# A first retention sequence re-laid as token pairs: all its matmuls in 64x64 quadrants

## The chip, the core and the metric

The kernel runs on one core of one Trainium2 chip. Five engines take part, each with its own instruction stream that is worked off in order: PE (TensorE, the matrix engine; its weight loads are shown apart as PEld), DVE (VectorE), ACT (ScalarE), POOL (GpSimd) and SP (SyncE, which here only issues DMA transfers). The metric is the device time of one execution in microseconds (us); the time before is the median of three runs. A profiled execution is a further one, with its own time.

## The reference

There are three stages, and the output is the last one's. B=2 sequences, H=8 heads, S=768 tokens, D=64; the middle width is 512, the hidden width 2048.

```python
state = zeros(B, H, D, D)
for t in range(S):                                        # retention
    state = gamma[h] * state + k[:, :, t] (outer) v[:, :, t]
    y[:, :, t] = q[:, :, t] @ state / sqrt(D)
x = y.transpose(0, 2, 1, 3).reshape(1536, 512)
h = x @ moe_w_in;   x = where(h > 0, h, exp(min(h, 0)) - 1) @ moe_w_out
h = x @ moe2_w_in;  out = (max(h, 0) + log1p(exp(-abs(h)))) @ moe2_w_out
```

The weights come as 64-bit floats, and the kernel turns them into 32-bit ones with integer steps on ACT and DVE.

## The kernel before

**Stages.** Retention is done in chunks of 128 tokens: chunks 0 to 5 are the first sequence, 6 to 11 the second. The first layer works on three blocks of 512 tokens (four chunks each); a block has 16 units, each of 12 matmuls into a hidden tile (`H`, line 517) and 12 out of it (`R`, line 558). Before block 0 can start, chunks 0 to 3 must be through: this is the head, 0 to 27.3 us. Chunks 4 to 11 are spread between the units of block 0 and block 1, and the weights of layer one are loaded and converted while block 0 runs (27 to 105 us). The second layer follows (lines 696 and 751).

**One chunk j of the first sequence.** q and k, 128 tokens by 512, are transposed on PE against an identity (`Tq`, `Tk`, line 370, four matmuls each) and copied out of PSUM (`tq` on DVE, `tk` on ACT). The decay of q is multiplied in either ahead of the transpose (j = 0 and 1: `dq`, line 360, DVE) or as it is copied out (j = 2 to 5: line 391, DVE). `S` (line 437, eight matmuls, 64 rows by 128 columns of the array) makes the scores; `m` (line 447, DVE, two instructions) masks them; `O` (lines 474 and 480) adds what the carried state gives to what the masked scores give; `ST` (line 417) makes the chunk's share of the state and `st` (lines 426 to 429, DVE) the next state, which `sp` (line 402, POOL) spreads over a zeroed tile `wide` so that line 474 can use the whole array. `dv` (POOL, line 363) decays v. `xh` (ACT) and `xl` (DVE) split the result in two for the first layer. Every fp32 matmul of the program is two instructions on PE: the trace says x16 where the program has eight.

**Order and queues.** The order on all engines is one written list of steps, `TABLE`; `ct`, `cl`, `cj`, `cs` in it convert one weight tile, `ih`, `il`, `oh`, `ol` split one, `ar` to `gl` are the activation of a unit, `kc` issues filler matmuls on PE (line 240). All loads are issued by SP in the list's order. In the head the steps take PSUM banks in turn from a ring of seven (`banks`), afterwards from two.

Of the kernel before, what the change touches and what calls it, by code (L numbers as in the profile page):

```python
# [20 lines left out]
DVE_TILES = 8  # L21
TABLE = """
ST.5 ST.11 sp.7 st.5 sp.6 sp.8 Tq.8 Tk.8 sp.9 Tq.9 Tk.9 sp.10 Tq.10 Tk.10 sp.11 Tq.11 Tk.11 st.11 Lq.0 Lk.0 Lk.1 Lq.1 Lv.0
Lv.1 Lk.2 Lq.3 dq.0 Lq.2 Tq.0 kc.3 Lg.0 tq.0 Tk.0 Lv.2 Tk.1 tk.0 tk.1 S.0 Lk.3 dq.1 Lv.3 Tq.1 dv.0 m.0 kc.2 ST.0 Lw.0 dv.1
tq.1 O.0 st.0 Lk.4 sp.1 S.1 xh.0 Lq.4 xl.0 Tk.2 Lw.1 m.1 ST.1 tk.2 Tq.3 Lw.2 Tq.2 st.1 O.1 tq.2 sp.2 Lv.4 tq.3 S.2 Lq.5 dv.2
xh.1 xl.1 Lw.3 dv.3 ST.2 m.2 Tk.3 tk.3 st.2 O.2 Lw.4 sp.3 ct.0 Lk.5 cl.0 S.3 xh.2 cj.0 Lv.5 xl.2 Tk.4 tk.4 m.3 Lg.1 cs.0 O.3
ct.1 ih.0 Lw.5 cl.1 il.0 few xh.3 ST.3 cj.1 dv.4 ct.2 xl.3 Tq.4 cl.2 cs.1 Lq.6 H.0 st.3 ih.1 tq.4 sp.4 Lw.6 il.1 cj.2 S.4
ct.3 cs.2 ar.0 Lw.7 ih.2 H.1 m.4 ae.0 cl.3 il.2 ct.4 dv.5 cl.4 ab.0 cj.3 Tq.5 gh.0 O.4 Lq.7 cj.4 ar.1 cs.3 ae.1 gl.0 Lw.8
oh.0 H.2 cs.4 xh.4 ol.0 ct.5 ab.1 ih.3 cl.5 tq.5 gh.1 il.3 R.0 Lb.64 ar.2 cj.5 ae.2 xl.4 ct.6 cs.5 cl.6 Lw.9 gl.1 oh.1 H.3
cj.6 ct.7 ol.1 cl.7 cs.6 ab.2 ih.4 cj.7 Tk.5 Lb.65 gh.2 ST.4 il.4 tk.5 R.1 ct.8 cs.7 cl.8 st.4 Lk.6 oh.2 gl.2 sp.5 ar.3 ol.2  # L30
ct.9 cj.8 cl.9 S.5 Lw.11 ae.3 Lw.10 cs.8 Lw.14 cj.9 H.4 ih.5 Lw.12 ab.3 cs.9 gh.3 Lv.6 m.5 oh.3 R.2 ol.3 ar.4 gl.3 Lw.13
ae.4 il.5 ct.11 ab.4 cl.11 R.3 gh.4 cj.11 gl.4 ct.10 cl.10 cs.11 Lk.7 cj.10 oh.4 Tk.6 cs.10 H.5 tk.6 ol.4 Lw.16 ih.6 il.6
Lw.15 dv.6 O.5 ar.5 ae.5 ab.5 H.6 ct.13 Lb.66 cl.13 ct.12 cj.13 cl.12 cs.13 Lv.7 xh.5 cj.12 gh.5 R.4 oh.5 xl.5 ct.14 cs.12
cl.14 Lb.67 ol.5 ih.7 gl.5 ar.6 Tq.6 il.7 ct.15 tq.6 Lw.17 ae.6 H.7 cj.14 cl.15 dv.7 ab.6 ct.16 cs.14 gh.6 Lb.68 cj.15 ih.8
S.6 gl.6 cl.16 il.8 ar.7 R.5 Lw.18 cs.15 ae.7 Lw.19 m.6 oh.6 Lw.20 ct.17 ab.7 cl.17 Lb.69 ol.6 gh.7 H.8 cj.16 cj.17 cs.16
cs.17 ih.9 O.6 gl.7 ct.18 il.9 oh.7 cl.18 ol.7 ST.6 ar.8 cj.18 Lb.70 xh.6 R.6 st.6 ae.8 cs.18 ct.19 xl.6 ih.10 ab.8 Lw.22
# [15 lines left out]
R.21 ae.23 il.25 ct.35 m.10 ab.23 H.24 gh.23 oh.23 gl.23 ol.23 O.10 ar.24 ih.26 ae.24 il.26 ab.24 ST.10 xh.10 gh.24 R.22
xl.10 st.10 gl.24 H.25 oh.24 ol.24 R.23 ar.25 ih.27 ae.25 il.27 ab.25 H.26 gh.25 oh.25 gl.25 ol.25 R.24 ar.26 ih.28 ae.26
il.28 ab.26 H.27 gh.26 oh.26 gl.26 ol.26 S.11 ar.27 ih.29 R.25 ae.27 il.29 m.11 ab.27 H.28 gh.27 oh.27 gl.27 ol.27 O.11 end
yh.0.0 ar.28 yl.0.0 ih.30 ae.28 il.30 yh.0.1 ab.28 R.26 xh.11 yl.0.1 gh.28 xl.11 gl.28 H.29 oh.28 ol.28 R.27 ar.29 ih.31
ae.29 il.31 ab.29 H.30 gh.29 oh.29 gl.29 ol.29 R.28 ar.30 ih.32 ae.30 il.32 ab.30 cs.32 H.31 gh.30 oh.30 Lw.36 gl.30 cl.34
# [65 lines left out]
def tile_retention_elu_softplus(  # L122
# [708 lines left out]
```

## Time and profile before

| | us |
|---|---|
| median of three runs (lowest, highest) | 576.35 (576.28, 576.6) |
| the profiled execution | 576.78 |
| its span, first to last instruction | 575.1 |
| PE busy in it | 568.2 |
| DVE, ACT, POOL busy in it | 451.9, 371.7, 27.9 |

A busy share is a mean over the whole span; what a stage is bound by is read from the stage. Matmuls overlap in the engine, so the length of one is no measure of its cost: the cost of a group is the distance from its start to the start of the next. In the chain of waits that distance stands as the length of a piece.

### The profile page before, as it was taken

Reading aid. Unit: us, or ns where it says so; the run is one execution under the profiler, and the core shown is the slowest. Engines: PE = TensorE matmul, PEld = TensorE weight load, DVE = VectorE, ACT = ScalarE, POOL = GpSimd, SP = SyncE. Lnnn points to the kernel's source line nnn. Section 1 sums busy time; section 2 is a strip of 40 time slices with the busy share of each in tenths; the row PEclk is TensorE's granted clock in tenths of the full one; section 3 lists DMA queues with packets and bytes.
Section 4 is the critical chain, followed back from the end, with each engine's and each line's share of the span. In section 5 each row is a group of like instructions: output and inputs, shape, how many; then the busy total and the mean of one; then the engine's idle time right before and its main releaser. Section 6 shows DMA issues by size and latency. Waiting matters only on the chain.

```text
span 575.1 us, 8682 instructions
## 1 busy us (share of the span) xinstructions
PE 568.2 (99%) x3236; PEld 484.8 (84%) x3236; DVE 451.9 (79%) x785; ACT 371.7 (65%) x678; POOL 27.9 (5%) x37
## 2 busy tenths in 40 slices
PE   8999999999999999999999999999999999999997
PEld 5888888788888888888888998998998988998995
DVE  3899899996566466999999999877789876666653
ACT  2588888865565455888999875545566655554442
POOL 3221202020010000000000000000000000000000
PEclk9999999999999999999999999999999999999999
DMA  9997676732270001406776000000000200000002
GB/s 199 270 293 218 179 217 169 207 60 53 40 191 2 0 1 55 129 0 190 217 219 216 2 1 0 1 0 2 0 1 0 111 2 0 1 1 1 0 1 109
DMA packets 75834, 48.29 MB, mean 84 GB/s; under 512 B 53520, under 2 KB 69904, under 8 KB 75792
## 3 DMA queue, kind: packets, MB, share of 16 engines
q1 hardware_dynamic: 75504, 47.46, 30.4%
q8 instruction: 25, 0.41, 0.3%
q10 hardware_dynamic: 288, 0.28, 0.1%
q14 instruction: 17, 0.14, 0.1%
HBM read 44.58 MB, written 3.15 MB: 83 GB/s over the span
## 4 chain that ended last, share of the span: by engine, by line
PE 89%; DVE 5%; ACT 2%; DMA 2%; issue 1%; DVEq 0%; ACTq 0%
PE psb L751 23%; PE psb L696 21%; PE psb L558 20%; PE psb L517 20%; PE psb L437 2%; PE psb L370 1%; DVE cl L284 1%; DVE wl L306 1%; DMA raw<-moe_w_out 1%; PE psb L417 1%; DVE wi L293 1%; ACT wh L300 1%; DMA early<-q 1%; DVE wo L293 1%; DVE A L447 1%
## 5 line engine op out<-in xcount | busy, mean ns | idle before, releaser
L751 PE MATMUL psb<-wo,g 128*128 128x512 f32 x576 | 142.1, 392 | 0.0
L751 PEld LDWEIGHTS psb<-wo,g 128*128 128x128 f32 x576 | 107.5, 188 | 19.4
L517 PE MATMUL psb<-x,wh 128*128 128x512 f32 x384 | 96.0, 392 | 0.8 <-DVE st L428 0.6
L517 PEld LDWEIGHTS psb<-x,wh 128*128 128x128 f32 x384 | 71.5, 188 | 16.5 <-ACT cl L279 1.0
L696 PE MATMUL psb<-op,wx 128*128 128x384 f32 x336 | 67.0, 339 | 0.0
L696 PEld LDWEIGHTS psb<-op,wx 128*128 128x128 f32 x336 | 60.2, 188 | 2.5
L306 DVE TENSOR_TENSOR wl<-wi,wh 128x512 fp32r<-128x512 f32 x48 | 32.9, 685 | 32.9 <-ACT wh L300 32.8
L721 ACT ACTIVATE hx<-hx 128x384 f32<-128x384 f32 x64 | 33.2, 520 | 37.5 <-DVE hx L717 37.4
L558 PE MATMUL psb<-gh,wh 128*128 128x512 f32 x192 | 56.0, 398 | 0.0
L558 PE MATMUL psb<-gh,wl 128*128 128x512 f32 x192 | 54.4, 390 | 0.0
L558 PE MATMUL psb<-gl,wh 128*128 128x512 f32 x192 | 54.3, 389 | 0.0
L517 PE MATMUL psb<-x,wl 128*128 128x512 f32 x192 | 51.3, 389 | 0.0
L525 ACT ACTIVATE e<-psb 128x512 f32<-128x512 f32 x48 | 28.3, 589 | 30.2 <-PE psb L517 30.1
L274 ACT ACTIVATE cm<-raw 128x512 f32<-128x512 f32 x64 | 42.6, 665 | 5.1 <-DVE wi L293 2.9
L731 ACT ACTIVATE g<-hx 128x384 fp32r<-128x384 f32 x64 | 33.2, 520 | 19.0 <-DVE hx L725 18.9
L284 DVE SCALAR_TENSOR_TENSOR cl<-cm,cl 128x512 int32<-128x512 int32 x64 | 43.8, 693 | 2.0 <-ACT cl L279 1.9
L669 DVE TENSOR_TENSOR wo<-wo,wo 128x512 fp32r<-128x512 f32 x32 | 22.0, 687 | 29.6 <-ACT wo L665 29.6
L536 ACT ACTIVATE gh<-e 128x512 fp32r<-128x512 f32 x48 | 30.1, 628 | 21.4 <-DVE e L532 21.2
L279 ACT ACTIVATE cl<-raw 128x512 int32<-128x512 uint32 x64 | 42.5, 664 | 1.6 <-DVE wi L293 1.1
L558 PEld LDWEIGHTS psb<-gh,wl 128*128 128x128 f32 x192 | 36.1, 188 | 7.6
L558 PEld LDWEIGHTS psb<-gl,wh 128*128 128x128 f32 x192 | 36.0, 188 | 7.5
L517 PEld LDWEIGHTS psb<-x,wl 128*128 128x128 f32 x192 | 36.1, 188 | 7.5
(102 smaller groups left out, 894.0 us busy)
## 6 DMA issues: line engine op xcount, KB each, us to landing
raw<-moe_w_in SPq DMA_DIRECT2D x32, 512.0 KB, 4.7
raw<-moe_w_out SPq DMA_DIRECT2D x32, 512.0 KB, 4.4
out_dram<-o SPq DMA_DIRECT2D x11, 256.0 KB, 2.1
early<-q SPq DMA_DIRECT2D x4, 256.0 KB, 4.9
early<-k SPq DMA_DIRECT2D x4, 256.0 KB, 5.0
early_v<-v SPq DMA_DIRECT2D x4, 256.0 KB, 5.1
qb<-q SPq DMA_DIRECT2D x64, 16.0 KB, 2.0
qb<-k SPq DMA_DIRECT2D x64, 16.0 KB, 1.9
```

What stands on the lines that cost most here:

```text
L274: nc.scalar.activation(out=m, in_=raws[i][:, :, :, 1].bitcast(F32), func=AF.Copy, scale=2.0 ** -112)
L279: nc.scalar.activation(out=l, in_=raws[i][:, :, :, 0].bitcast(U32), func=AF.Copy, scale=2.0 ** -29 * (1 - 2.0 ** -12), bias=-0.499)
L284: nc.vector.scalar_tensor_tensor(out=l, in0=m.bitcast(I32), scalar=3, in1=l, op0=ALU.logical_shift_left, op1=ALU.bitwise_or)
L306: nc.vector.tensor_tensor(out=l, in0=wf[f][o], in1=ws[u, o][0].bitcast(F32), op=ALU.subtract)
L517: nc.tensor.matmul(b, w[:, kk, :], x[:, kk, :], start=(n == 0), stop=(n == len(seq) - 1))
L525: nc.scalar.activation(out=e, in_=hb[u], func=AF.Relu, scale=-1.0)
L536: nc.scalar.activation(out=gh, in_=acts[u], func=AF.Copy)
L558: nc.tensor.matmul(acc[i], st[:, i * P:(i + 1) * P], mv, start=(fresh and p == 0), stop=(f == NF - 1 and p == 2))
L696: nc.tensor.matmul(bank_p[b], w[:, h, k], x[l][:, k], start=(start and i == 0), stop=(i == len(seq) - 1), skip_group_check=True)
L721: nc.scalar.activation(out=e, in_=e, func=AF.Softplus)
L731: nc.scalar.activation(out=t[:, 0], in_=hid[Q, c][1], func=AF.Copy)
L751: nc.tensor.matmul(sums2[s], t[:, x, i * P:(i + 1) * P], o[:, w], start=(left[s] == 0 and p == 0), stop=(left[s] == 2 * NQ - 1 and p == 2) ...
```

## The change

It touches chunks 0 to 5 alone, and the order of everything.

- **Layout.** q, k and v of the first sequence are loaded so that one partition holds two neighbouring tokens of four heads (partitions 0 to 63 heads 0 to 3, the others heads 4 to 7). The pieces in memory are 512 bytes, before 256; each tile is two DMAs instead of one.
- **Quadrants.** `Tq`, `Tk`, `S`, `O` and `ST` are matmuls of 64 rows by 64 columns of the array, written so that four neighbours in the order fall on its four quarters. `Tq` and `Tk` are now plain matmuls, 16 for each tile, k against a folded identity `fold`, q against `scale_q`, the same with q's decay in it, made once (`dq`, DVE). `dq` of chunks 0 and 1 and the multiplication of line 391 are gone for the first sequence; `tq` of chunks 1 to 5 is two plain copies of half the size on ACT.
- **State.** The state needs no `wide`: `sp` is gone, and the state's part of `O` is two groups of four matmuls, one ahead of time (`X`) and one in `O`. `ST` writes into the same two banks as `O`. A tiny DVE copy `y` (128x4, `seen`) stands between `X` and `O`.
- **Halves.** `m` and `O` are split in halves, so that the first half of `O` can follow the first half of `m`.
- **Banks.** In the head the steps take pairs of banks by the list `PAIRS`. The pair (h0, h1) is among them; H.0 and H.1 write there.
- **Fillers.** The five later filler matmuls are gone, the first seven remain. `TABLE` is new throughout.

```diff
-            nc.sync.dma_start(out=t, in_=src)
+            src = heads.rearrange("(g h) (p e) d -> g p h (e d)", g=2, e=2)
+            for g in range(2):
+                nc.sync.dma_start(out=t[g * D:(g + 1) * D].rearrange("p (h e) d -> p h (e d)", e=2), in_=src[g])
...
+PAIRS = (0, 2, 4, 6, 0, 2, 4, 6, 0, 2, 6, 4, 0, 2, 4, 6)
...
-    def decay_query(j):
-        nc.vector.tensor_tensor(out=qkv[0, j], in0=qkv[0, j], in1=gt, op=ALU.mult)
+    def decay_diagonals():
+        nc.vector.tensor_tensor(out=scale_q, in0=fold.unsqueeze(1).to_broadcast([P, H, D]), in1=rates(H + HP, H), op=ALU.mult)
...
+        if j < CPB:
+            key = ("t", j, n if j == 0 else 0)
+            first = key not in bank
+            b = bank[key] if not first else pair(key)
+            for c in range(HP):
+                for g in range(2):
+                    for a in range(2):
+                        r, o, h = slice(g * D, (g + 1) * D), a * D, HP * a + c
+                        nc.tensor.matmul(b[o:o + D, g, (n * HP + c) * D:(n * HP + c + 1) * D], qkv[n, j][r, h, :],
+                                         fold[r] if n else scale_q[r, h, :], start=(first and c == 0), stop=(c == HP - 1), skip_group_check=True)
...
+                if j:
+                    for g in range(2):
+                        nc.scalar.activation(out=x[:, g], in_=y[:, g], func=AF.Copy)
+                else:
+                    nc.vector.tensor_copy(x, y)
...
-    def spread_state(j):
-        if j % CPB and j < CPB:
-            for i in range(2):
-                r = slice(i * D, (i + 1) * D)
-                nc.gpsimd.tensor_copy(wide[j % 2][r, :, r], states[j][r])
...
+    def carry(j, x):
+        b, qT = bank["o", j], qkT[0, j]
+        for a in range(2):
+            for c in range(2):
+                r, i = slice(a * D, (a + 1) * D), a ^ x
+                nc.tensor.matmul(b[c * D:(c + 1) * D, i, a * P:(a + 1) * P], states[j][r, 2 * i + c, :], qT[r, 2 * i + c, :],
+                                 start=(x == 1), stop=False, skip_group_check=True)
...
+    def settle(j):
+        x = seen[j] = rp.tile([P, 2, 2], F32, tag="seen", name="seen")
+        nc.vector.tensor_copy(x, bank["o", j][:, :, 0:2 * P:P])
```

What the new list makes of the order is seen at three places. The first is PE's stream around chunk 2's output in the head. `early` and `early_v` are the tiles that hold the loaded q, k, v and the transposed q and k of chunks 2 and 3, `wide` and `st` the state, `A` the masked scores, `psb` PSUM; the counts are those of the program. Before:

```order
L370 MATMUL psb<-ident,early 128x128 x8
L474 MATMUL psb<-qT,wide 128x128 x4
L480 MATMUL psb<-A,early_v 64x128 x8
L437 MATMUL psb<-early_v 128x128 x8
L417 MATMUL psb<-early_v,early 64x64 x8
L370 MATMUL psb<-ident,early 128x128 x4
L474 MATMUL psb<-early_v,wide 128x128 x4
```

And now:

```order
L488 MATMUL psb<-qT,st 64x128 x4
L555 MATMUL psb<-A,early_v 64x128 x16
L448 MATMUL psb<-early_v,early 64x64 x16
L507 MATMUL psb<-early_v 64x128 x16
L488 MATMUL psb<-early_v,st 64x128 x4
L390 MATMUL psb<-fold,early 64x64 x16
L390 MATMUL psb<-scale_q,early 64x64 x16
```

Where the state's matmuls stood together ahead of the scores' (line 474, 480), the state's are now four ahead of the next chunk's transposes and four behind them, and the next chunk's scores (line 507) follow the state's share at once.

The second place is PE's stream where the first layer begins (line 517 before, 592 now; `x_234` and `x_350` are block 0's tokens, `wh` and `wl` the two parts of a weight tile). Before:

```order
L474 MATMUL psb<-early_v,wide 128x128 x4
L480 MATMUL psb<-A,early_v 64x128 x8
L417 MATMUL psb<-early_v,early 64x64 x8
L370 MATMUL psb<-ident,q 128x128 x4
L517 MATMUL psb<-x_234,wh 128x512 x4
L517 MATMUL psb<-x_234,wl 128x512 x4
L517 MATMUL psb<-x_234,wh 128x512 x4
L437 MATMUL psb<-qT,kT 128x128 x8
```

And now:

```order
L390 MATMUL psb<-scale_q,q 64x64 x16
L488 MATMUL psb<-early_v,st 64x128 x4
L555 MATMUL psb<-A,early_v 64x128 x16
L448 MATMUL psb<-early_v,early 64x64 x16
L507 MATMUL psb<-qT,kT 64x128 x16
L488 MATMUL psb<-qT,st 64x128 x4
L592 MATMUL psb<-x_350,wh 128x512 x4
L592 MATMUL psb<-x_350,wl 128x512 x4
```

The scores of chunk 4 (line 437, now 507) and the first half of its carried part stood behind H.0 and now stand ahead of it.

The third place is DVE's stream in the head from chunk 2 on (`cl` and `cm` belong to the conversion of a weight tile, `wi` is its result). Before, from `tq` of chunks 2 and 3 on:

```order
L391 TENSOR_TENSOR early_v<-psb,gq_94 128x512 x2
L499 TENSOR_TENSOR x_234<-psb,x_234 128x4x128
L447 TENSOR_TENSOR A<-psb,mask 128x512 x2
L428 TENSOR_TENSOR st<-psb,st 128x256
L429 TENSOR_TENSOR st<-st,dec 128x256
L284 SCALAR_TENSOR_TENSOR cl<-cm,cl 128x512
```

And now, from the mask of chunk 3 on:

```order
L523 TENSOR_TENSOR A<-psb,mask_e 128x512
L572 TENSOR_TENSOR x_350<-psb,x_350 128x4x128
L497 COPY seen<-psb 128x4
L298 SCALAR_TENSOR_TENSOR cl<-cm,cl 128x512
L523 TENSOR_TENSOR A<-psb,mask_e 128x512
L307 SCALAR_TENSOR_TENSOR wi_122<-raw,cl 128x512
```

The multiplication of q is gone from it, the halves of the mask stand apart, and two steps of the weights' conversion stand between and behind them.

## Rows read from the trace of the kernel before

**Rows 1.** The page, part 1: busy time, share of the span and instructions by engine
```profile
PE 568.2 (99%) x3236; PEld 484.8 (84%) x3236; DVE 451.9 (79%) x785; ACT 371.7 (65%) x678; POOL 27.9 (5%) x37
```

**Rows 2.** Busy times by stage, its length first, cut where the text cuts
```profile
core 0: us, PE busy (x) PEld busy (x) DVE busy (x) ACT busy (x) POOL busy (x), PEclk, DMA share, GB/s
0.00:9.25 9.25, 7.25 (x24) 3.86 (x24) 2.35 (x4) 1.88 (x2) 2.46 (x11) 1.00 0.96 176
9.25:27.30 18.05, 17.86 (x247) 15.46 (x247) 13.16 (x23) 7.68 (x14) 6.54 (x10) 1.00 1.18 254
27.30:105.30 78.00, 77.19 (x529) 62.63 (x529) 75.36 (x121) 65.29 (x117) 11.33 (x10) 1.00 0.78 216
105.30:209.00 103.70, 103.70 (x703) 84.74 (x704) 70.08 (x113) 60.18 (x110) 7.59 (x6) 1.00 0.30 69
```

**Rows 3.** Who PE waited for, whole run, microseconds, times, longest
```profile
PE psb L370 <- DVE early L360: 0.7, 1, 0.7
PE psb L517 <- DVE st L428: 0.6, 1, 0.6
PE psb L437 <- DVE qT L391: 0.2, 1, 0.2
```

**Rows 4.** The chain that ended last, first 110 us: start, length, what
```profile
0.81 3.51 DMA early<-q
...
7.54 1.71 PE psb L370 x8
9.25 1.09 PE psb L437 x16
...
14.55 0.62 PE psb L417 x16
...
16.19 0.89 PE psb L474 x8
17.08 1.02 PE psb L480 x16
...
34.61 0.44 PE psb L370 x4
```

**Rows 5.** PE in order of time at 100 us: start, length, work
```profile
99.77 0.67 PE L459 MATMUL psb<-qT,st 64*64 64x128 f32 x16
100.26 0.41 PE L463 MATMUL psb<-A,v 64*64 64x64 f32 x16
100.60 0.69 PE L466 MATMUL psb<-A,v 128*64 128x64 f32 x16
```

**Rows 6.** PE in order of time at the head
```profile
1.26 3.17 PE L240 MATMUL psb<-warm 128*128 128x512 bf16 x7 [1.26 <-DVE warm L234]
...
9.18 1.16 PE L437 MATMUL psb<-qT,kT 64*128 64x128 f32 x16
...
27.26 1.20 PE L517 MATMUL psb<-x,wh 128*128 128x512 f32 x4 [0.18 <-ACT x L495]
```

**Rows 7.** VectorE in order of time at the head
```profile
10.44 1.29 DVE L447 TENSOR_TENSOR A<-psb,mask 128x512 f32<-128x512 f32 x2 [1.80 <-PE psb L437]
...
15.79 0.42 DVE L429 TENSOR_TENSOR st<-st,dec 128x256 f32<-128x256 f32 x1
16.22 1.29 DVE L391 TENSOR_TENSOR early_v<-psb,gq 128x512 f32<-128x512 f32 x2
```

**Rows 8.** Groups by line to 105 us, VectorE first, then ScalarE
```profile
L360 DVE TENSOR_TENSOR early<-early,dec 128x512 f32<-128x512 f32 x2 | 1.4, 692 | 4.1 <-DMA early<-q 4.1
L389 DVE COPY qT<-psb 128x512 f32<-128x512 f32 x2 | 1.4, 685 | 1.3 <-PE psb L370 1.3
...
L387 ACT ACTIVATE kT<-psb 128x512 f32<-128x512 f32 x6 | 3.6, 592 | 7.9 <-PE psb L370 7.9
```

**Rows 9.** Two stretches of the head, the DMA rate last
```profile
5.00:12.00 7.00, 6.83 (x57) 5.16 (x59) 2.97 (x6) 1.19 (x2) 2.08 (x2) 1.00 1.32 219
27.00:32.00 5.00, 4.58 (x31) 3.51 (x31) 4.93 (x9) 3.13 (x6) 2.54 (x3) 1.00 1.15 297
```

More of the change, by code (lines that the diff above doesn't have):

```diff
@@ L27 @@
[L27 to L36, printed above, removed]
@@ L52 @@
[L52 to L56, printed above, removed]
@@ L210, in tile_retention_elu_softplus @@
     dec = const.tile([P, 3 * H + 2 * HP], F32, name="dec")
-    gq = [const.tile([P, HP * P], F32, name=f"gq{n}") for n in range(2)]
+    gq = const.tile([P, HP * P], F32, name="gq")
+    scale_q = const.tile([P, H, D], F32, name="scale_q")
     nc.scalar.dma_start(out=dec, in_=decay)
@@ L318, in psum @@
     def psum(tag):
-        assert tag not in live
+        assert tag not in live, (tag, live)
         return psb[:, names.index(tag)]
-    banks = ["h0", "h1", "a0", "a1", "a2", "r0", "r1"]
+    banks = []
+    pairs = list(PAIRS)
     turn = [0]
@@ L349, in release @@
         return bank.pop(key)
-    wide = [rp.tile([P, HP, P], F32, tag="qb", name="wide") for i in range(2)]
-    for w in wide:
-        nc.gpsimd.memset(w, 0.0)
     qkT = {}
@@ L423, in next_state @@
         s = rp.tile([P, HP, D], F32, tag="st", name="st")
-        bb = release(("s", j))[:, 0:HP * D].rearrange("p (h d) -> p h d", h=HP)
+        if j < CPB:
+            bb = bank.pop(("s", j)).rearrange("p i (c d) -> p i c d", c=2)
+            out, old, rate = (None if x is None else x.rearrange("p (i c) d -> p i c d", i=2)
+                              for x in (s, states.get(j), dec[:, H:H + HP].unsqueeze(2).to_broadcast([P, HP, D])))
+            users[j] -= 1
+            if not users[j]:
+                release(("o", j))
+        else:
+            bb = release(("s", j))[:, 0:HP * D].rearrange("p (h d) -> p h d", h=HP)
+            out, old, rate = s, states.get(j), gs[1]
@@ L442, in causal @@
         if j < TPB:
-            a = [gp.tile([P, HP, P], F32, tag=t, name="A") for t in ("gh", "gl")]
+            a = gp.tile([P, HP, P], F32, tag=("gh", "gl")[i], name="A")
         else:
-            a = [ap.tile([P, HP, P], F32, tag=t, name="A") for t in ("A0", "A1")]
-        for i in range(2):
-            nc.vector.tensor_tensor(out=a[i], in0=bs[i].rearrange("p (h t) -> p h t", h=HP),
-                                    in1=(mask_t if i and j >= CPB else mask).unsqueeze(1).to_broadcast([P, HP, P]), op=ALU.mult)
@@ L449, in causal @@
-        scores[j] = a
-    def attend(j):
+            a = ap.tile([P, HP, P], F32, tag=("A0", "A1")[i], name="A")
+        m = mask_e.rearrange("p k t -> p (k t)") if j < CPB else mask_t if i else mask
+        n = 2 if j < CPB else HP
+        nc.vector.tensor_tensor(out=a.rearrange("p (c k) t -> p c (k t)", c=n), in0=bs[:, i].rearrange("p (c t) -> p c t", c=n),
+                                in1=m.unsqueeze(1).to_broadcast([P, n, HP // n * P]), op=ALU.mult)
+        scores.setdefault(j, []).append(a)
@@ L452, in attend @@
+    def attend(j, half=0):
         vt, qT = qkv[2, j], qkT[0, j]
-        a = scores.pop(j)
+        a = scores[j]
+        b = bank.get(("o", j)) if j in seen or half else pair(("o", j))
+        users[j] = 1
         if j >= CPB:
-            b = pair(("o", j))
             quads = [(i, pr, pr % 2 * D, pr // 2 * P) for n in range(0, HP, 2) for i in range(2) for pr in (n, n + 1)]
```

324 lines of the change are left out of this document (189 added, 135 removed).

## The prediction

> **What bounds the kernel now.** The views were read in this order. The page's busy times first: PE is busy 568.2 us of a span of 575.1 [rows 1], so the time is PE's work plus some 7 us. The table by stage next: between 27.3 and 105.3 us PE is busy 77.2 of 78.0, but DVE also 75.4 and ACT 65.3; from 105.3 to 209 us PE is alone, DVE has 70 of 104 [rows 2]. Then PE's waits: apart from the start there are three, 0.7 us before the first transpose, 0.6 us for a state of the second sequence (this one is at 105 us), 0.2 us for a transposed q behind H.0 [rows 3]. So the kernel ends when PE's work ends, DVE is close behind PE until 105 us, and a microsecond less of PE work counts fully only where DVE and ACT can follow. The profiled execution took 576.78 us, 1.68 more than its span; the median of the runs is 576.35. I sum against 576.78 and take the difference off 576.35.
>
> **Prices of the quadrant matmuls.** The second sequence already has them: 16 instructions of 64x64 with 128 columns take 0.49 us from their start to the next group's (99.77 to 100.26), 16 with 64 columns 0.34 (100.26 to 100.60) [rows 5]. Behind the second the shape of the array changes, behind the first it doesn't. I take 0.44 for the first, a little under the row since the 0.49 has a shape change at its own start. For the second the bounds are 0.22 (half, by columns) and 0.34 (the row); I take 0.235, near the lower one, since at the end of the 0.34 PE goes over to another shape, and inside the head this no longer happens: all groups are 64x64.
> Per chunk, in calls of two instructions each:
> - transposes of q and k: before 2 x 0.44 where nothing else is paid (34.61), more at most places [rows 4]; now 32 calls, 64 instructions with 64 columns, 4 x 0.235 = 0.94. Nothing gained, perhaps 0.1 lost.
> - scores: before 1.09 [rows 4]; now 16 calls with 128 columns, 0.87. Gain 0.2.
> - output: before 0.89 + 1.02 [rows 4]; now 8 calls for the state (0.44) and 16 for the scores (0.87). Gain 0.6.
> - state: before 0.62 [rows 4]; now 16 calls with 64 columns, 0.47. Gain 0.15.
> So 4.5 us a chunk become 3.6. It is the joined shapes and the half-empty `wide` that pay, not the transposes.
>
> **The head, followed as a chain.** With less PE work the head is no longer filled by PE; I follow the waits by hand. From PE's last score matmul to the mask DVE needs 0.1 us behind the row's end (9.18 + 1.16 to 10.44), that is 0.3 us after PE could go on; two masks take 1.29, `st` with both its steps 0.9 (to 16.22), a plain ACT copy 0.6 [rows 6, 7, 8]. Before, S.0 starts at 9.18 and H.0 at 27.26 [rows 6].
> Now: the fillers end at 4.2 [rows 6], k's first tile is there by then (the first q, 256 KB, landed at 4.3 when it was first in the queue [rows 4]; now a tile is two halves and k is ahead). Two transposes at the slow pace, 0.94 each, end at 6.2; `scale_q` is made meanwhile and hides behind Tk.0. tq.0 on DVE 6.55 to 7.25, S.0 at 7.3. From there each chunk needs 3.6 us of PE plus what it waits: X.j waits for `st` of the chunk before, which ends 1.2 us after ST while S.j covers 0.87 of it, so 0.3 to 0.4 us are lost a chunk. That puts S.1 at 11.1, S.2 at 14.8, S.3 at 18.8 (allowing 0.3 for a slow S.0). In the fourth round two things are added. Tk.4 takes the pair of banks that xl.2 still reads, and on DVE xl.2 stands behind st.2 and the first mask of chunk 3: PE waits until 21.3. And m.3.1, st.3 and xl.3 stand behind conversion steps of the first weights on DVE: O.3 ends at 23.4, ST.3 at 23.8, S.4 at 24.7, X.4 waits for st.3 until 25.1, and H.0, which writes the bank that o.3 lies in, waits for xl.3, until 26.3. Against 27.26 that is 0.95 us earlier, with more done: S.4 and half of chunk 4's carry already lie behind it.
>
> **Behind H.0.** Before, PE still has of the first sequence S.4 1.09, O.4 1.91, ST.4 0.62, the transposes of chunk 5 0.9, S.5 1.09, O.5 1.91: 7.5 us. Now: the rest of O.4 1.09, ST.4 0.47, transposes 0.94, S.5 0.87, X.5 and O.5 1.3: 4.7. Gain 2.8. The shape changes towards the first layer's matmuls are about as many as before (S.4, O.4, ST.4, S.5, O.5 against X.4, O.4 with ST.4, transposes, S.5, O.5), so they count zero. The two waits behind H.0, 0.2 and 0.6, fall away if DVE keeps up: gain 0.8.
>
> **Can DVE and ACT follow?** DVE loses two `dq` of 0.69, one of two copies of line 389, and four multiplications of line 391 (0.65 each from the pair), and gains `scale_q` and five tiny copies, which I bound by zero and 0.4 each and take at 0.15 [rows 7, 8]: about 3 us less. ACT gains five `tq`, between 0.6 and 0.8 each: 3.5 us. DVE had 2.6 us of slack in the 78 us to 105.3 [rows 2]; PE will need some 74.4 us for the same stretch, DVE about 74.4 of work. That is tight, but DVE starts it with work already done: in the head it was idle 11.7 of 27.3 us [rows 2], and the weights come earlier, since the loads of 256-byte pieces ran at 219 GB/s with the DMA engines full, and the mixed stretch later at 297 [rows 9]; for pieces of 512 bytes I take between the two. Following R.0 to H.5 by hand I find PE not waiting. I allow 0.4 us (bounds 0 and 3).
>
> **POOL and SP.** `sp` and `wide` go from POOL, two masks come; all hidden, v's decay now has POOL to itself. SP issues 18 DMAs more; the first ones took 0.43 us each to issue, and 36 halves at that price are as fast as the data, so zero, with 1 us as the worst.
>
> **Sum.** 0.95 + 2.8 + 0.8 - 0.4 = 4.2 us. 576.78 - 4.2 = 572.6 for the profiled execution, 576.35 - 4.2 = 572.2 us for the median.
>
> **Rivals.**
> 1. The head overlaps better than my chain (waits of 0.3 vanish, Tk.4 and H.0 aren't held by xl.2 and xl.3). Then PE's work alone counts: 15 us from S.0 at 7.3, H.0 at 22.3 to 23.5. Gain up to 3 us more: 569. For it: DVE and ACT have room in the head; against: the two bank waits are in the program.
> 2. The gain turns into waits on DVE and ACT before 105 us. For it: DVE is 97% busy there and ACT gets more [rows 2]; against: the idle head. Price: PE gains no more than DVE sheds, 2 to 3 us less a late conversion: 574.5.
> 3. Small quadrants are bound by issue and weight loads, not by columns: 0.34 for 16 everywhere [rows 5]. Twelve transposes and five states at 0.2 us more each are 3.5 us on PE, about 2.5 of them on the path: 574.5. A sentence from the Trainium skill, "TensorE: Matmul & The Clock Gate" (Wait — 56ns, not 53.3ns?), says that start-to-start never drops below about 25 ns however few the columns; an estimate from it is 0.8 us for each 32 instructions, which would take the whole gain. Here 16 starts take 0.34, 21 ns each with the shape change in it, so the trace doesn't bear it out.
> 4. Slower: the clock. The granted-clock column reads 1.00 throughout [rows 2], yet eight transposes took 1.71 us at 7.54, 0.21 each, and four took 0.44 later, 0.11 each [rows 4]: until about 9.2 us PE ran at the pace of the 1.2 GHz level, then at that of 2.4. Before it rose PE had been busy without a gap since 5.2, with three fillers in it. Now it has gaps of 0.3 to 1.1 us from 6.2 on and no fillers. If the pace stays low, each chunk has 2.7 us more on the chain; after a chunk and a half (at about S.2) the gain is gone, and through the whole head it costs 8 to 12 us: 580. Against it: the fillers now run straight into the transposes, 1.3 to 6.2 without a gap.
>
> **How the numbers follow.** Forecast (570.5 to 573.8) 0.48; rival 1 0.17; rival 2 0.17; rival 3 0.07; rival 4 0.11. A measurement tells about 0.2%, 1.15 us, from no change. Faster by more, under 575.2: the forecast, rival 1, most of 2, half of 3, 0.81. Within: the ends of 2 and 3 and a short rival 4, 0.10. Slower: the rest of rival 4, 0.09. The range leaves out rival 4 and the ends of 1 and 2: 568.5 to 575.8.
>
> **What would show it.** Right: S.0 near 7.3, S.1 to S.3 at steps of 3.7 to 4.0, H.0 at 26 to 27 with a wait for xl.3 before it, groups of 0.87 for the scores, transposes of 0.47, and no PE wait over 0.5 us between 27 and 100. Wrong: transposes of 0.65, scores that still take 1.7 us beyond 10 us, PE waiting for DVE lines 298 to 320 between 40 and 70 us, or H.0 at 23.

## The result: slower, and where the time went

The changed kernel takes 584.72 us (median of 4 runs, 584.07 to 586.3) against 576.48 of the kernel before on the same chip, a ratio of 1.0146 (95% interval 1.0122 to 1.017). The forecast was 572.2, with a range of 568.5 to 575.8: it has the wrong sign. The profiled execution took 585.34. Each run below has one profiled execution, and what is read from a trace is that execution's.

The page of the changed kernel, its first lines (engine, busy us, share, instructions), against [rows 1]:

```profile
span 583.3 us, 9981 instructions
PE 566.3 (97%) x3879; PEld 484.2 (83%) x3879; DVE 448.1 (77%) x784; ACT 373.0 (64%) x688; POOL 22.6 (4%) x29
```

PE's work fell by 1.9 us, and the span grew by 8.2. H.0, the first layer's first group, starts at 36.65 instead of 27.26 us [rows 6]. So the span is cut there. This is the table by stage, with columns as in [rows 2], of the kernel before, from the end of the fillers on:

```profile
4.20:27.26 23.06, 22.13 (x263) 18.39 (x262) 15.20 (x26) 8.24 (x15) 6.54 (x10) 1.00 1.20 246
27.26:575.00 547.74, 543.09 (x2968) 465.54 (x2968) 436.40 (x759) 362.21 (x663) 18.92 (x16) 1.00 0.27 77
```

and of the changed kernel:

```profile
4.20:36.65 32.45, 22.40 (x793) 20.11 (x792) 13.85 (x28) 11.52 (x24) 4.18 (x5) 0.89 0.78 222
36.65:583.28 546.63, 540.95 (x3080) 463.18 (x3080) 433.25 (x755) 360.22 (x664) 15.17 (x12) 1.00 0.26 74
```

Behind H.0 the new kernel is 1.1 us shorter, with 2.1 us less of PE's work. Ahead of it, it is 9.4 us longer: PE is busy just as long (22.4 against 22.1), in three times as many matmuls (793 against 263), and idle 10.0 us instead of 0.9. So the work isn't what grew there, but the waiting. What it waited for there (engine, line, what it waited for: us in total, times, longest):

```profile
PE psb L390 <- DMA early<-q: 2.6, 3, 1.2
PE psb L507 <- issue: 1.9, 1, 1.9
PE psb L448 <- issue: 1.7, 1, 1.7
PE psb L390 <- DMA early<-k: 1.0, 1, 1.0
PE psb L390 <- DVE x L572: 1.0, 1, 1.0
PE psb L507 <- DVE qT L424: 0.9, 1, 0.9
PE psb L592 <- DVE x L572: 0.8, 1, 0.8
```

and from H.0 on (the first of these three is at 129 us, the second the one ahead of H.0):

```profile
PE psb L592 <- DVE e L607: 1.4, 1, 1.4
PE psb L592 <- DVE x L572: 0.8, 1, 0.8
PE psb L488 <- DVE seen L497: 0.3, 1, 0.3
```

Two waits of the head are odd. "issue" means that PE waited for nothing that the profile shows, and both stand in the middle of a group, where no semaphore is awaited. This is the timeline of PE around them (start, us, engine, line, operation, count, idle before it in brackets):

```profile
23.89 0.72 PE L507 MATMUL psb<-early_v 64*64 64x128 f32 x18
26.49 0.55 PE L507 MATMUL psb<-early_v 64*64 64x128 f32 x10 [1.88 <-issue]
...
31.80 0.27 PE L448 MATMUL psb<-early_v,early 64*64 64x64 f32 x3
33.78 0.63 PE L448 MATMUL psb<-early_v,early 64*64 64x64 f32 x27 [1.71 <-issue]
```

The DMA queues say what PE ran out of. Part 3 of the page has, beside the data's queues, two of kind "instruction", of which one, q14, moves nothing in this stretch. Up to 36.6 us the row of the other (packets, MB, share) reads in the kernel before

```profile
q8 instruction: 2, 0.03, 0.5%
```

and in the changed one

```profile
q8 instruction: 6, 0.10, 1.3%
```

Each packet is 16,384 bytes, and the page counts 30 in the whole run:

```profile
q8 instruction: 30, 0.49, 0.4%
```

The trace has 7,803 recorded instructions of TensorE (matmuls, weight loads and a few others), 260 for each packet, so a packet looks like one block of 256 instructions. Counted in order, the two stops lie ahead of numbers 1217 and 1473, exactly 256 apart. The first of the two blocks came from 24.23 to 25.23 us and PE went on at 26.48; the second from 31.34 to 32.48, PE went on at 33.78.

Where such a packet runs, data is late. In the head, the 16 parts of a load of q, k or v land within 0.4 to 1.0 us of each other when none runs. The three halves that PE waited longest for are three during which such a packet ran: the second half of q of chunk 1 (parts from 9.22 to 11.71; packet 8.59 to 10.45), of q of chunk 2 (14.44 to 16.53; 14.38 to 15.46) and of k of chunk 3 (19.53 to 21.31; 18.60 to 19.62). And SyncE's DMA issues, 0.616 us each in the median, take 1.6 to 2.0 us when one falls in with them. The timeline of SyncE's queue, two issues to a row:

```profile
7.51 1.27 SPq L185 DMA_DIRECT2D early_v<-v  x2
8.82 2.69 SPq L185 DMA_DIRECT2D early<-k  x2
11.56 1.28 SPq L185 DMA_DIRECT2D early<-q  x2
12.88 1.28 SPq L185 DMA_DIRECT2D early_v<-v  x2
14.20 2.27 SPq L185 DMA_DIRECT2D early<-q  x2
```

The chain of waits seems to tell another story. It follows SyncE's issues up to 20.76 us and then the weight tile w1 (start, length, what):

```profile
20.76 6.06 DMA raw<-moe_w_in
26.91 0.68 ACT cm L288
27.61 0.69 DVE x L572
28.35 1.99 PE psb L390 x64
```

But line 572 here is xl.2, which reads PSUM and the result of xh.2 and no weight; xh.2 (ACT, line 568) had started at 24.56 and took 0.60. On DVE it stands behind the mask m.3.0 (line 523), and starts 0.61 us after it, DVE's usual distance between two such instructions:

```profile
27.00 0.69 DVE L523 TENSOR_TENSOR A<-psb,mask_e 128x512 f32<-128x512 f32 x1 [2.02 <-PE psb L507]
27.61 0.68 DVE L572 TENSOR_TENSOR x<-psb,x 128x512 fp32r<-128x512 f32 x1
```

The mask waited for the scores of chunk 3 (line 507), the group that the first stop cut in two. ACT's work on w1 merely ended at the same moment. So the first stop lies on the way to H.0, through the mask, xl.2 and Tk.4; and so does the second, through ST.3, st.3 and xl.3.

### The profile page after: what moved, and what is told of

Its sections match the earlier page's. It is cut to its first block, busy times and chain, and to the rows that moved or that the text cites. A ratio compares the mean times of both kernels' runs of the same rounds, so it can differ in the third digit from the quotient of the medians.

```text
span 583.3 us, 9981 instructions
## 1 busy us (share of the span) xinstructions
PE 566.3 (97%) x3879; PEld 484.2 (83%) x3879; DVE 448.1 (77%) x784; ACT 373.0 (64%) x688; POOL 22.6 (4%) x29
## 4 chain that ended last, share of the span: by engine, by line
PE 93%; SPq 3%; DMA 1%; DVE 1%; issue 1%; ACT 0%; DVEq 0%; ACTq 0%
PE psb L633 23%; PE psb L592 23%; PE psb L826 22%; PE psb L771 20%; SPq L185 3%; PE psb L512 1%; DMA raw<-moe_w_in 1%; PE psb L543 1%; PE psb L390 1%; PE psb L536 1%; PE psb L555 1%; PE psb L456 0%; DMA out_dram<-o 0%; PE psb L395 0%; PE psb L488 0%
## 5 line engine op out<-in xcount | busy, mean ns | idle before, releaser
L320 DVE TENSOR_TENSOR wl<-wi,wh 128x512 fp32r<-128x512 f32 x48 | 33.3, 695 | 25.9 <-ACT wh L314 25.7
L298 DVE SCALAR_TENSOR_TENSOR cl<-cm,cl 128x512 int32<-128x512 int32 x64 | 45.1, 709 | 2.6 <-ACT cl L293 2.5
L744 DVE TENSOR_TENSOR wo<-wo,wo 128x512 fp32r<-128x512 f32 x32 | 22.1, 690 | 30.3 <-ACT wo L740 30.2
L810 DVE TENSOR_TENSOR g<-hx,g 128x384 fp32r<-128x384 f32 x64 | 35.4, 555 | 10.7 <-ACT g L806 10.7
L740 ACT ACTIVATE wo<-wo 128x512 fp32r<-128x512 f32 x32 | 20.1, 632 | 34.7 <-PE psb L826 34.6
```

The source lines that it names most:

```text
L298: nc.vector.scalar_tensor_tensor(out=l, in0=m.bitcast(I32), scalar=3, in1=l, op0=ALU.logical_shift_left, op1=ALU.bitwise_or)
L320: nc.vector.tensor_tensor(out=l, in0=wf[f][o], in1=ws[u, o][0].bitcast(F32), op=ALU.subtract)
L810: nc.vector.tensor_tensor(out=t[:, 1], in0=hid.pop((Q, c))[1], in1=t[:, 0].bitcast(F32), op=ALU.subtract)
```

## The experiments

Four views stood against each other. A: SyncE's issue of twice as many DMAs paces the head. B: the slow clock. C: TensorE's instructions, 352 a chunk instead of 128, come too slowly. D: the new order of banks. (The counts include the weight load that goes with each matmul. In the kernel before a transpose is one matmul instruction, as its `x4` for four shows, and not two like the others: 8 and 56 matmuls a chunk, 176 now.)

**Halves issued by two engines.** The second halves of chunks 0 to 3 go to ScalarE's queue.

```diff
-            for g in range(2):
+            for g in range(1 if j < TPB else 2):
                 nc.sync.dma_start(...)
+    def load_act(n, j):
+        nc.scalar.dma_start(out=t[D:].rearrange("p (h e) d -> p h (e d)", e=2), in_=src[1])
```

> The changed kernel, but the second half (partitions 64 to 127) of each load of the first four chunks is issued by ScalarE, some places ahead of its use, and only the first half by SyncE. Theory A (SyncE's issue of one 128 KB half every 0.66 us paces the head): S.1 (13.5 us in the changed kernel) comes at 11 to 12, S.2 (18.5) at 15, w1 (issued at 20.8) is issued before 14, H.0 (36.65) starts at 28 to 31, and the time falls by 4 to 7 us, to 578 to 581. Theory C (TensorE itself stops in the head because its instructions, twice as many as before, come in too slowly): the stops of 1.9 and 1.7 us inside groups stay, H.0 moves by under 3 us, time 582 to 585. Theory D (the order of banks: Tk.4 behind xl.2, H.0 behind xl.3): H.0 moves only as far as xl.3 does, both waits stay.

588.72 us, ratio 1.0198 (1.0181 to 1.0214): slower still, H.0 at 40.65. w1 was issued at 12.2 us, before 14 as A had it, and H.0 came no earlier. Yet it is no clean test of A, since ScalarE's issues themselves waited, and its copies of k and q behind them: PE waited 2.4 us for one copy of q, 1.4 for another and 2.4 for a load of k. But the stops "issue" were there again, 1.3 and 1.2 us, now ahead of instructions 449 and 705; these are 256 apart, and 705 + 2 x 256 is the 1217 of the changed kernel.

**The kernel before with its loads in halves.**

```diff
-            nc.sync.dma_start(out=t, in_=src)
+            for g in range(2):
+                nc.sync.dma_start(out=t[:, g * HP:(g + 1) * HP], in_=src[:, g * HP:(g + 1) * HP])
```

> The kernel before, with each load of the first sequence cut into two DMAs of 128 KB (four heads each, pieces of 256 bytes as before); TensorE's program is unchanged. Theory A: SyncE needs 0.6 us or more for each half, so the 13 loads up to w0 take until 17 to 18 instead of 14.3, w1 is issued at 21 to 23 instead of 18.3, H.0 starts at 30 to 33 instead of 27.26, and the time rises by 3 to 5 us to 579 to 582. Theory C: no change of more than 0.5 us, since TensorE fetches as many instructions as before. A third view, that SyncE only waited for full DMA queues in the kernel before (issues of 1.0 to 1.1 us where the first took 0.43), would also leave the time where it is: halves of 0.6 us are then as fast as the data.

577.86 against 577.4, ratio 1.0006 (0.9995 to 1.0018); H.0 at 28.26. Twice the DMAs cost nothing that the time shows. An issue took 0.51 us here, and the loads of the first four chunks landed as early as before (k of chunk 3 at 17.5 us, 18.0 before); w1 landed at 25.9 us, 23.95 before, and H.0 came 1.0 us later. So the doubling as such is not the cause. The 0.616 us of an issue to 64 partitions is not tested by this; the next run bounds what late loads can cost.

**Without the loads of chunks 1 to 3.**

```diff
+        if 0 < j < TPB:
+            qkv[n, j] = qkv[n, 0]
+            return
```

> The changed kernel without the loads of chunks 1, 2 and 3 of the first sequence: these chunks use chunk 0's q, k and v again, and v's decay is applied once only, so their results are those of other data; every other instruction of TensorE, VectorE and ScalarE stays. It shows what the head takes when its data never comes late. Theory A: no wait for a DMA behind chunk 0, the groups follow each other at 3.6 us a chunk, and H.0 waits for w1 or starts at 22 to 25. Theory C: TensorE still stops for 1 to 2 us inside groups, at the 1217th and the 1473rd of its recorded instructions, where it stopped in the changed kernel, and H.0 comes no earlier than 28 or so. Theory B (the clock): with no gaps the granted clock is 1.00 from 8 us on.

582.37 us in one run, H.0 at 33.97: with q, k and v of these chunks never late, the head is still 6.7 us longer than before. So taking the late loads away gives back 2.7 of the 9.4 us, and A falls as the main cause. The timeline of PE:

```profile
7.73 1.10 PE L512 MATMUL psb<-qT,kT 64*64 64x128 f32 x32 [0.89 <-DVE qT L429]
8.63 0.67 PE L395 MATMUL psb<-fold,early 64*64 64x64 f32 x32
9.09 0.68 PE L395 MATMUL psb<-scale_q,early 64*64 64x64 f32 x32
9.72 1.22 PE L560 MATMUL psb<-A,early_v 64*64 64x128 f32 x32
10.76 0.52 PE L453 MATMUL psb<-early_v,early 64*64 64x64 f32 x22
14.70 0.58 PE L453 MATMUL psb<-early_v,early 64*64 64x64 f32 x9 [3.42 <-issue]
...
27.19 0.54 PE L512 MATMUL psb<-early_v 64*64 64x128 f32 x10 [1.06 <-issue]
```

The quadrants run at the forecast prices (scores 0.90, transposes of k 0.46), and then PE stands for 3.4 us with all its data there: ahead of instruction 449, whose block came from 12.19 to 13.35. Here the weights w0 to w4 were under way instead. Both stops, 3.4 and 1.1 us, stand in this run's own chain of waits: 4.5 of the 6.7 us. The slow clock follows the stop, it doesn't lead. In this table by stage of the run the last column but two is the granted clock, 1.00 and then 0.58:

```profile
4.20:12.00 7.80, 6.19 (x215) 5.43 (x214) 1.98 (x3) 1.75 (x4) 1.06 (x2) 1.00 0.92 254
12.00:20.00 8.00, 5.30 (x136) 5.26 (x140) 2.40 (x5) 1.33 (x3) 0.00 (x0) 0.58 0.68 205
```

**Half the instructions, everything else as it is.** The first sequence's matmuls read the upper halves of their operands as bf16, one pass instead of two.

```diff
+    def hi(x):
+        return x.bitcast(BF16)[:, 1::2]
-    qkv[n, j][r, h, :], fold[r] if n else scale_q[r, h, :]
+    hi(qkv[n, j][r, h, :]), hi(fold[r] if n else scale_q[r, h, :])
     (and so in score, carry, attend, state)
```

> The changed kernel, but TensorE's work on the first sequence (transposes, scores, carried state, values, states) reads only the upper halves of its float32 operands as bf16: the same 64x64 quadrants, loads, copies and order, but one pass instead of two, so half the matmuls and half the weight loads (the first sequence's results lose precision). Theory C (256 instructions of TensorE come in one transfer of 16 KB, and the head runs out of them): with some 176 instead of 352 instructions a chunk there is no stop inside a group before H.0, three or four transfers instead of six by then, and H.0 starts at 27 to 30 instead of 36.65, set by q, k and the weights; time 574 to 579. Theory A' (SyncE's halves alone set the head): TensorE's shorter work changes little, the waits for DMA q and k stay or grow by as much, H.0 stays at 34 to 36.5, time 582 or more.

579.83 us in one run. H.0 starts at 30.12, 6.5 us earlier than in the changed kernel, with two packets of instructions by then, and no "issue" among PE's waits from the fillers to H.0; the longest are

```profile
PE psb L393 <- DMA k<-k: 4.0, 2, 3.7
PE psb L393 <- DMA early<-q: 3.9, 4, 1.5
```

This also speaks against B. The granted clock was low here for most of the head, and H.0 came earlier all the same:

```profile
12.00:20.00 8.00, 4.96 (x167) 3.71 (x159) 4.89 (x11) 2.69 (x8) 1.32 (x2) 0.50 0.74 213
```

**The same with each matmul twice**, so that the number of instructions is that of the changed kernel again.

```diff
+    def twice(*args, start=False, **kw):
+        nc.tensor.matmul(*args, start=start, **kw)
+        nc.tensor.matmul(*args, start=False, **kw)
```

> The one-pass kernel (upper halves as bf16) with each of its matmuls on the first sequence issued twice, so that TensorE has as many instructions as in the changed kernel, 352 a chunk, but of bf16 (every sum is taken twice, so the results are multiples). Loads, copies and order are those of the one-pass kernel, whose H.0 started at 30.12. Theory C (the number of instructions): stops of 1 us or more inside groups come back, five or six transfers before H.0, H.0 at 34 to 38. If the two passes of float32 cost their time otherwise than by their number: no such stop, H.0 within 1.5 us of 30.12.

586.29 us in one run, H.0 at 36.70, six packets by then, and the stops are back, ahead of 1217 and 1473 as in the changed kernel. PE's timeline (L251 is the line of the helper):

```profile
28.39 0.33 PE L251 MATMUL psb<-early_v 64*64 64x128 bf16 x4 [4.32 <-issue]
...
33.89 0.28 PE L251 MATMUL psb<-early_v,early 64*64 64x64 bf16 x4 [1.43 <-issue]
36.70 1.65 PE L599 MATMUL psb<-x,wh 128*128 128x512 f32 x3 [0.77 <-DVE x L579]
```

Same loads, same copies, same order, same type of operand: doubling the instructions moves H.0 by 6.6 us, and the stops come and go with their number. The pair alone doesn't part the supply of the instructions from the time that the doubled matmuls take themselves: between the fillers and H.0 PE was busy 18.3 us here and 12.9 in the one-pass kernel. That the stops belong to the supply is seen from their place, at the edges of the blocks of 256, PE going on 1.3 to 1.5 us behind a packet; and the kernel before, with 22.1 us of PE's work in its head, has H.0 at 27.26.

**More instructions in the kernel before.** Scores, states and values are cut into two of half the columns, 240 instructions a chunk.

```diff
-    kT[i * D:(i + 1) * D, pr, :], qT[i * D:(i + 1) * D, pr, :]
+    for x in range(0, P, D): ... kT[i * D:(i + 1) * D, pr, :], qT[i * D:(i + 1) * D, pr, x:x + D]
     (and so in state, attend)
```

> The kernel before, with every matmul of the first sequence's scores, states and values cut into two of half as many columns: the same loads, columns, copies and order, and 240 instead of 128 instructions of TensorE a chunk. Theory C: TensorE stops once or twice inside a group before H.0, or its data and SyncE's issues are held up by more transfers of instructions (five instead of two before H.0), and H.0 starts 2 to 5 us later than 27.26, beyond what the split matmuls themselves take longer (read from their groups' rows); time 578 to 582. Theory A' (the changed kernel lost its time to the number of DMAs or to their pieces): H.0 moves only by what the split groups take longer, no stop inside a group, and by under 1 us in the time if they run at half the price each.

586.8 us, ratio 1.0162 (1.0144 to 1.018), H.0 at 33.44, and yet not a single stop inside a group: C's expectation missed. The whole price is PE's own (it idles for 1.0 us between 4.2 and 33.0 us), since halves of these shapes cost nearly as much as wholes:

```profile
7.59 2.05 PE L441 MATMUL psb<-qT,kT 64*128 64x64 f32 x32 [0.16 <-ACT kT L387]
17.23 1.90 PE L479 MATMUL psb<-qT,wide 128*128 128x64 f32 x16
```

(To the next group's start 1.98 and 1.82 us; 16 scores took 1.09 before, 8 of line 474 0.89 [rows 4].) At that pace 256 instructions last 6.8 us, longer than a packet takes to come. So it isn't the number as such but the number in a time: in these runs the supply shows only where instructions are as short as a 64x64 quadrant's.

**Fewer transposes.** q and k are transposed by 128x64 matmuls, 288 instructions a chunk.

```diff
-    nc.tensor.matmul(b[o:o + D, g, ...], qkv[n, j][r, h, :], fold[r] if n else scale_q[r, h, :], ...)
+    nc.tensor.matmul(b[a * D:(a + 1) * D, c // 2, x:x + P], qkv[n, j][:, HP * a + c, :], ident if n else scale_q[:, HP * a + c, :], ...)
```

> The changed kernel with the transposes of the first sequence as 128x64 matmuls against a 128x128 diagonal (q's decay still in it) instead of 64x64 quadrants: 64 instead of 128 instructions of TensorE a chunk for q and k, 288 instead of 352 in all; the copies of k come as two of half the size on ScalarE, and the diagonal takes VectorE 1.2 instead of 0.6 us. Theory C: one transfer of instructions fewer by H.0, one stop fewer, H.0 at 33 to 35.5 although the transposes themselves take a little longer, time 580 to 583.5. If transposes' own length counted more than their number, H.0 would move later by 1 to 3 us, time 586 to 588.

584.82 (1.0135; 1.0111 to 1.016), no gain, where C had expected 580 to 583.5; H.0 at 37.65, in an execution of 587.14. One stop less, but the one left was 2.5 us, ahead of 961: its packet began 4.8 us after PE had reached the block before, with v of chunk 3 and w1 under way.

**Weights held back**, and both together (with chunk 4's k and q ahead of w1).

```diff
-  ... xh.3 S.4 Lw.2 il.0 ... m.4.0 Lw.3 Lw.4 ct.3
+  ... cl.1 Lx.2 Lx.3 tk.4 ... xh.3 Lx.4 S.4 il.0 ... m.4.0 ct.3      (Lx: load_w on ScalarE's queue)
```

> The changed kernel, but the weight tiles w2, its partner w3 and w4 are issued by ScalarE behind its reads of w1 (from about 28 us on) and behind xh.3, instead of by SyncE at 24.0 to 26.2 us; nothing else moves. In the changed kernel the transfer of instructions that TensorE needed from its 1473rd instruction on began at 31.3 us, 4.9 us after it had begun the block before, with these three tiles (1.5 MB) under way. If that transfer waits behind data that was issued ahead of it: it begins by 29 us, the stop of 1.7 us inside the state's group goes, H.0 starts at 34.5 to 35.5 instead of 36.65, time 582 to 584. If the transfer's lateness has nothing to do with the data: the stop stays at 1.5 us or more, and H.0 stays within 0.5 us.

> The wide transposes (288 instead of 352 instructions of TensorE a chunk), with w2, w3 and w4 held as in the run beside it, and chunk 4's k and q issued ahead of w1. With fewer instructions and less data ahead of their transfers: at most one stop of over 0.5 us inside a group before H.0, H.0 at 31 to 34, time 579 to 582.5. If neither matters: H.0 at 37 and 584 to 585 as with the wide transposes alone.

Held: 585.11 (1.0136; 1.0117 to 1.0155). The packet for 1473 began at 29.0 instead of 31.3 and its stop is gone, H.0 is at 35.88; but there were stops of 0.4, 1.4 and 2.0 us ahead of 705, 961 and 1217, of which the changed kernel had only the last. Up to 24 us the two programs issue the same, so the stops differ from one execution to the next, and one trace doesn't give their size exactly. Both: 583.92 (1.0114; 1.0099 to 1.0129), H.0 at 33.02, one stop of 0.8 us. The granted clock was 1.00 through this head, which is still 5.8 us longer than before: against B once more. The head gained 3.6 us on the changed kernel, but from H.0 to the end of the span it took 549.2 us instead of 546.6, so most of it was given back; that the late weights did this is likely, and was not tested apart. That data under way delays the packets is suggested by the packet for 1473 and not shown by these two; holding back what is needed soon after is no cure.

**No data under way at all.** The loads of chunks 1 to 3 left out as above, and w0 to w4 held.

```diff
+  ... Lv.3 tk.3 Lx.0 Lx.1 xl.1 ... xh.3 Lx.2 Lx.3 Lx.4 S.4
```

> The run without the loads of chunks 1 to 3 (which use chunk 0's q, k and v again), and in addition w0 and w1 are issued by ScalarE only behind chunk 3's copy of k and w2, w3 and w4 behind xh.3, so that from some 10 us until then no data is under way at all. TensorE's program is that of the changed kernel. If the transfers of its instructions are late because they wait behind data: those for the blocks that begin between 10 and 20 us start within 0.7 us of TensorE's reaching the block before (1.0 to 4.9 us in the changed kernel), no stop inside a group there is longer than 1 us, and S.3, which the run without the loads started at 25.3 us and the changed kernel at 23.8, starts before 21.5. If the lateness is in the transfers' own mechanism: delays of 1 to 4 us and stops of 1 us or more stay.

584.88 us in one run. H.0 starts at 31.43, but H.1 behind it waits for late weights until 37.16, so the time says nothing here. From 11 to 20 us the DMA queues hold this and nothing else:

```profile
DMA packets 2, 0.03 MB, mean 4 GB/s; under 512 B 0, under 2 KB 0, under 8 KB 0
q8 instruction: 2, 0.03, 1.3%
```

and PE's timeline still has

```profile
15.79 0.97 PE L560 MATMUL psb<-A,early_v 64*64 64x128 f32 x25 [0.59 <-issue]
...
23.48 0.54 PE L512 MATMUL psb<-early_v 64*64 64x128 f32 x10 [1.06 <-issue]
```

Both theories missed in part, S.3 starting at 21.6: the delay is neither all data's nor all its own. With no data under way, a packet begins 1.2 to 1.7 us after PE reaches the block before (0 to 4.9 in the changed kernel, 3.9 in the run without loads), takes 0.9 to 1.0, and PE goes on 1.3 to 1.5 us after its end. The packets began at 13.43, 17.12 and 21.23, and PE went on at 15.79, 19.51 and 23.47 (data runs again from 21.4). So where TensorE has to stop for each block, it gets 256 instructions in 3.7 to 4.0 us. In the stops of the other runs below, with data under way, the packet began 2.5 to 4.9 us after the block before was reached; that the data is the reason is likely, and not shown, since other packets began early with data under way too. My count of stops, packets and restarts, in us:

| run | block from instruction | PE reached the block before | packet | PE went on | stop |
|---|---|---|---|---|---|
| changed kernel | 1217 | 21.7 | 24.23 to 25.23 | 26.48 | 1.9 |
| changed kernel | 1473 | 26.5 | 31.34 to 32.48 | 33.78 | 1.7 |
| without loads | 449 | 8.3 | 12.19 to 13.35 | 14.70 | 3.4 |
| each matmul twice | 1217 | 21.7 | 25.58 to 26.94 | 28.39 | 4.3 |
| no data | 705 | 12.2 | 13.43 to 14.36 | 15.79 | 0.6 |
| no data | 1217 | 19.5 | 21.23 to 22.19 | 23.47 | 1.1 |

**What is left over: 30.12 against 27.26.** The one-pass kernel with chunk 4's k and q ahead of w1.

```diff
-  Lw.1 ct.0 m.3.0 ... ct.1 Lk.4 xl.2 Lq.4 Tk.4
+  Lk.4 Lq.4 Lw.1 ct.0 m.3.0 ... ct.1 xl.2 Tk.4
```

> The one-pass kernel (upper halves as bf16, half of TensorE's instructions on the first sequence, less precise) with chunk 4's k and q issued ahead of w1 instead of behind it. The one-pass kernel's H.0 started at 30.12, 2.9 us later than in the kernel before, and its longest wait was one of 3.7 us for chunk 4's k, which landed at 24.9 to 25.4 us (21.7 in the kernel before, where it is issued ahead of w1). If the order of these loads makes most of what the number of instructions leaves over: that wait falls under 1.5 us, H.0 starts at 27.5 to 29, time 577 to 579. If something else then holds H.0 (w1's conversion, the slow clock): H.0 stays at 29.5 or later, time 579.5 or more.

580.39 (1.0057; 1.0037 to 1.0076), H.0 at 30.98. This is the second of the two outcomes. The wait for k is gone, and in its place PE waits 2.4 us for xl.2 and 2.5 us for chunk 4's copies of k and q, which stand on ScalarE behind the conversion of w1. w1 now lands at 26.75 us; in the kernel before it was there at 23.95. So what is left over looks like the loads' pace: SyncE gave out 128 KB each 0.66 us, 199 GB/s, and the DMA engines were 0.71 to 0.77 busy up to 20 us at 196 to 218 GB/s, where the kernel before had them full and moved 246. Whether the issues, the 64-partition halves or the slow clock in that run (0.50 from 12 to 28 us) weigh most in these 3 us stays open.

No version ran that beats the kernel before. The one that the runs point to, the old head with quadrants only behind H.0, could win about the 1.1 us measured there, 0.2%; it needs a second layout of heads and wasn't tried.

## Why the prediction was wrong, by its steps

- **Prices of the quadrants: right.** 0.90 and 0.46 in the rows of the run without loads, for forecasts of 0.87 and 0.47. Rival 3 (0.34 for 16 everywhere) falls: 32 starts in 0.46 us are 14 ns each. The Trainium skill's sentence from "TensorE: Matmul & The Clock Gate" (Wait — 56ns, not 53.3ns?), no start-to-start under some 25 ns, doesn't hold for four quadrants at once; the measurement decides.
- **The step that failed: "From there each chunk needs 3.6 us of PE plus what it waits."** The forecast priced a chunk's matmuls by columns (64 for the transposes, 176 in all by its calls) and put the delivery of the instructions, 352 with the weight loads, at nothing without a reason. At 256 in 3.7 to 4.0 us, the measured pace without data, they need an estimated 5.1 to 5.5 us a chunk, against 3.6 of PE and 4.5 in the kernel before, whose 128 need about 2.0 and so never show. Forecast S.1 to S.4 at 11.1, 14.8, 18.8 and 23.8; measured 13.5, 18.5, 23.8 and 34.2. In the first rounds the waits that show are those for loads, 3.6 us in all, 3.2 of them with a packet of instructions under way; in the last round they are the two stops, 1.9 and 1.7 us. Without the late loads the stops grew to 4.5 us and 6.7 of the 9.4 us stayed. Half the instructions with the same loads took 6.5 of the 9.4 us away, but this includes the matmuls' own time, which was halved too; how much is the delivery's alone no run tells.
- **"36 halves at that price are as fast as the data, so zero": wrong in the changed layout.** The price taken, 0.43, was that of the first issue; 64-partition halves took 0.66 with the gap between them. That the doubling itself is free held for the kernel before (1.0006). How much of the 2.9 us that the one-pass kernel leaves over is due to this stays open; moving chunk 4's loads forward gained nothing there. The forecast's "weights come earlier" fell with it: w1 landed at 26.8 instead of 23.95.
- **Bank waits: right**, Tk.4 behind xl.2 (1.0 us) and H.0 behind xl.3 (0.8), as forecast, and tq.0 (0.9). D is true and was in the sum.
- **Behind H.0: right in kind, too large.** 2.8 us less of PE's work forecast, 2.1 measured, and 1.1 in the time. The waits of 0.6 and 0.2 [rows 3] did go, but 1.4 us came anew between 120 and 150 us, in the stretch that the forecast left to PE alone, and 0.3 for the settled banks. DVE and ACT did follow up to 105 us, against rival 2.
- **Rival 4, the clock, had the right sign (580) by the wrong cause.** The granted clock, the last column but two, fell twice in the head of the changed kernel:

```profile
8.00:10.00 2.00, 2.00 (x57) 2.00 (x55) 0.43 (x1) 0.00 (x0) 1.04 (x1) 0.50 0.70 196
28.00:30.00 2.00, 1.65 (x60) 1.66 (x64) 2.00 (x5) 0.14 (x1) 0.00 (x0) 0.50 1.03 386
```

  It was 0.79 from 10 to 12 and 0.67 from 30 to 32 us, and 0.93 or more otherwise. S.0 took 1.74 us to the next group instead of 0.90, chunk 4's transposes 1.76 instead of 0.92, 1.7 us for the two. The slow stretches come behind waits and stops. What the clock alone costs was not tried; that it isn't the main cause is seen from the one-pass kernel (0.50 from 12 to 28 us, and faster) and from the wide transposes with the weights held (1.00, and still 5.8 us behind in the head).
- **Two small readings.** By [rows 2] DVE was idle 11.8 us of the head, not 11.7, and PE had a further wait of 0.2 us, for xh.3 ahead of H.0 [rows 6]. Nothing hangs on either.

## What to carry to other kernels

Count TensorE's instructions per microsecond of a dense stretch, not its columns alone: cutting work into four small quadrants and two passes each multiplies them, and in the trace the packets of the instruction queue and stops "issue" inside a group, at a fixed distance in instructions, show that PE waits for them. Small quadrants pay where long matmuls stand between them (behind H.0), not in a head that has nothing else to issue. And try a layout in the one stretch that is to gain before a whole sequence is moved to it.

## What of the hardware was not expected

- TensorE's instructions come while the program runs, 16 KB for 256 of them, one packet after the other. Where TensorE stopped for each, with no data under way, it had 256 in 3.7 to 4.0 us; a packet began up to 4.9 us after the block before it was reached, in an execution with weights under way.
- Where such a packet ran, data was late: the parts of the three loads that PE waited longest for landed over 1.8 to 2.5 us instead of 0.4 to 1.0, and SyncE's issues at the same moments took 1.6 to 2.0 us instead of 0.6.
- Matmuls of 64x128 and 128x128 tiles on half the columns cost nearly the same each (32 scores 2.0 us, 16 had taken 1.1), where 64x64 quadrants with 64 columns start every 14 ns.
